# Asking earlier for the last weights of the first expert, and checking the counts later

## The chip, the core and the metric

The kernel runs on one core of one Trainium2 chip. The core has five engines with queues of their own: TensorE (PE in the rows; its weight loads are PEld), VectorE (DVE), ScalarE (ACT), GpSimd (POOL) and SyncE (SP), which here only issues transfers. Each engine takes its instructions in the order in which they were written into its queue, and waits on semaphores for what others produce. The metric is the device time of one execution in microseconds, the median of three runs.

## What is computed

Three stages follow each other, on 3072 tokens of 384 numbers: a linear attention with a decaying state, a gated MLP (`sigmoid(x @ w_gate) * (x @ w_val) @ w_out`), and a mixture of eight experts of which every token takes one. The change lies in the third:

```python
logits = xn @ en.T / tau
expert_idx = np.argmax(logits, axis=1)
gate_w = probs[np.arange(N), expert_idx]
for e in range(E):
    mask = expert_idx == e
    h = np.maximum(x[mask] @ w1[e], 0.0)
    out[mask] = gate_w[mask, None] * (h @ w2[e])
```

`w1[e]` is 384 by 1024 and `w2[e]` 1024 by 384, all in float32.

## The kernel before

Attention and MLP run over groups of 256 tokens. From the second third on two groups are taken together in a "wide" step of 512 columns (L720, L765). When a group's rows of x are done, each row is given an expert and a place in that expert's region of a DRAM buffer `xs`, and GpSimd scatters the rows there (`route_rank`, L837; two scatters of 128 rows for each group). An expert later reads its rows back from `xs` as one block.

The experts come after the last wide step. Their weights lie in DRAM as eight blocks f = 0 to 7 of 128 by 768: 384 columns of w1 and 384 of w2. `load_we` (L851) asks for one block, 384 KB, into one of three buffers `wraw`; `split_we` (L858 to L863) makes of it a high part (ScalarE) and a rest (VectorE), in a tile `we` of the pool `wp`. That pool has 18 places of 6 KB a partition, which held the MLP's weights before and are used anew as these are done with. The call `weights(e, f)` splits block f of expert e + 1 and asks for the block two further on. So a load waits for a free `wraw`, that is for the split three blocks earlier.

The first expert (expert 0) has 448 rows and is computed in pieces, so that the PE need not wait for the last four scatters. Its 320 early rows, which earlier groups filled, are read during the last wide step (tile `first`, `first_rows`): two tiles of 128 rows and one of 64. Their first layer is `first_h` (tiles `hm`, eight blocks f), run right after the last wide step, while the last two groups are ranked and scattered beside it. The second layer of the two whole tiles is `emit_y(0, f, 0)` and `emit_y(0, f, 1)` (L1332). The 64 early rows go through `emit_rest` (L1358): GpSimd adds the two parts of `hm` into `rh` (L1416), and eight products take the plain float32 weights w2 from two tiles `w2f` of 768 KB each, asked for by `load_rest` (L1342). The 128 late rows (tile `x0`, read by the transfer of L1424 after all scatters) are transposed (L1429), copied to `x0T` (L1430) and taken through both layers (L1435, then L1332 with t = 2) with plain float32 weights for the first. Then expert 1 begins, whose rows are the tile `xrow` (`load_rows`, L1277) and are transposed by `do_xT` (L1297).

`verdict` (L1189 to L1209) checks on VectorE whether the counts fit the regions and the decays lie in their range, with one small product on the PE, and writes a flag. A general path is taken at the very end if the flag is set; all engines read it there. SyncE's read of it (`TENSOR_LOAD flag`, L1486) may be placed earlier in its queue by the tile framework, which orders each engine's instructions by priorities of its own.

Of the kernel before, what the change touches and what calls it, by code (L numbers as in the profile page):

```python
# [8 lines left out]
F32 = mybir.dt.float32  # L9
F32R = mybir.dt.float32r  # L10
BF16 = mybir.dt.bfloat16
# [5 lines left out]
ALU = mybir.AluOpType  # L17
AX = mybir.AxisListType

CAP = 448  # L20
# [4 lines left out]
FIRST = 320  # L25
# [21 lines left out]
EMB_T = (-1.29,)  # L47
EMB_AT = 24.35
WARM = 12
VERDICT = 5  # L50
RANK = 1
DOTS = ((2, 3, 3, 2, 0, 0), (4, 4, 4, 4, 4, 4))
WARM_WIDE = 6
# [8 lines left out]
def kernel(  # L62
# [44 lines left out]
    def after_scatters(key, ins):  # L107
        ins = getattr(ins, "ins", ins)
        for q in scatters[key]:
            tc.add_manual_dep(  # L110
                ins, q.name, mybir.DependencyInfo(mybir.DependencyClass.Sync, mybir.DependencyReason.DATA),
                reason="reads what every scatter wrote",
            )

    def follow(ins, before):

        tc.add_manual_dep(
            ins, before.name,
            mybir.DependencyInfo(mybir.DependencyClass.NoSync, mybir.DependencyReason.DATA), reason="order",
        )  # L120
# [181 lines left out]
    if True:  # L302
# [546 lines left out]
        def load_we(e, f):  # L849
# [2 lines left out]
            wraw[e, f] = r  # L852
            last_we[:] = [getattr(q, "ins", q)]

        last_relu = []

        def split_we(e, f):
# [37 lines left out]


        fst = {}
        lim = c1.tile([P, 4, 4], F32, name="lim")
        left = lim[:, 3, 3:4]

        def first_rows():
            assert not dots and not ranks
            cum = cums[LAST % 3]
            pc = ps_a.tile([P, E], F32, tag="a0", name="pc")
            nc.tensor.matmul(pc, ones, cum[:, 0, :], start=True, stop=True)
            nc.vector.tensor_scalar(left, pc[:, 0:1], -1.0, float(FIRST), op0=ALU.mult, op1=ALU.add)
            nc.vector.tensor_scalar(left, left, 0.0, None, op0=ALU.max)
            experts_in_order(pc[0:1, :])
            for t in range(2):
                nc.vector.tensor_tensor(slot0[1][:, t, 0:1], slot0[1][:, t, 0:1], left, op=ALU.add)  # L910
            x = wp.tile([P, 3, RW], F32, tag="w", name="first")
            for a, b, n in ((0, 2, P), (2, 3, FIRST - 2 * P)):
                rows = xs[a * P:a * P + (b - a) * n].rearrange("(t p) c -> p t c", p=n)
                after_scatters("xs", nc.sync.dma_start(out=x[0:n, a:b], in_=rows))
            fst["x"] = x
            for q in range(2):
                r = wp.tile([P, 4, 384], F32, tag="w", name="raw1")
                nc.sync.dma_start(out=r, in_=wex[0, 4 * q:4 * q + 4, :, 0:384].rearrange("f p c -> p f c"))
                fst["w", q] = r
# [245 lines left out]
        for g, f, wide in steps:  # L1165
            if wide == 2:
                for _ in emit_wide(g, f):
                    at_tick()
                    tick += 1
            else:  # L1170
                emit_gv(g, f)
            pend.append((g, f, wide))
            at_tick()
            tick += 1
            drain(LAG if wide == 1 else 1)
            if g == LAST and f < 2:
                load_we(0, f)
            if g == LAST and f >= 2:
                split_we(0, f - 2) if f - 2 < XF else None
                if f < XF:  # L1180
                    load_we(0, f)
                elif f < XF + 2:
                    load_we(1, f - XF)
            if g == LAST and f == AT_ROWS:
                first_rows()
            if g == LAST and f >= 9:
                first_xT(f - 9)
        drain(0)
        def verdict():  # L1189
            q = nc.vector.tensor_scalar(lim[:, 0, :], wd, W_MIN, None, op0=ALU.is_ge)  # L1190
            follow(getattr(q, "ins", q), fst["lo"])
            nc.vector.scalar_tensor_tensor(lim[:, 1, :], wd, W_MAX, lim[:, 0, :], op0=ALU.is_le, op1=ALU.mult)
            nc.vector.tensor_reduce(lim[:, 2, 0:1], lim[:, 1, :], axis=AX.X, op=ALU.add)
            tot = c1.tile([P, E + 2], BF16, name="tot")
            nc.vector.tensor_copy(tot[:, 0:E], cums[NG % 3][:, 0, :])
            nc.vector.tensor_copy(tot[:, E:E + 2], lim[:, 2, 0:1].to_broadcast([P, 2]))
            pf = ps_a.tile([P, E + 2], F32, tag="a0", name="pf")
            nc.tensor.matmul(pf, ones, tot, start=True, stop=True)
            fl = lim[0:1, 3, :]
            nc.vector.tensor_tensor(fl[:, 2:3], pf[0:1, 0:1], left[0:1, :], op=ALU.add)  # L1200
            over = Am0[0:1, 6, 0:E]
            nc.vector.tensor_tensor(over, pf[0:1, 0:E], cape, op=ALU.subtract)
            nc.vector.tensor_reduce(fl[:, 0:1], over, axis=AX.X, op=ALU.max)
            nc.vector.tensor_scalar(fl[:, 0:1], fl[:, 0:1], 0.0, None, op0=ALU.is_gt)
            nc.vector.tensor_scalar(fl[:, 1:2], pf[0:1, E:E + 1], 4.0 * P, None, op0=ALU.is_lt)
            nc.vector.tensor_scalar(fl[:, 2:3], fl[:, 2:3], float(CAP), None, op0=ALU.is_gt)
            nc.vector.tensor_tensor(fl[:, 0:1], fl[:, 0:1], fl[:, 1:2], op=ALU.max)
            nc.vector.tensor_tensor(fl[:, 0:1], fl[:, 0:1], fl[:, 2:3], op=ALU.max)
            nc.vector.tensor_copy(flag, fl[:, 0:1])  # L1209

        tiles = [(g, t, xr) for g, xr in ends for t in range(2)]
        turned = []
        for f in range(XF):
            first_h(f)
            if f == 0:
                turned = [route_turn(xr, t, n) for n, (g, t, xr) in enumerate(tiles)]
            elif f == 1:
                for n, (g, t, xr) in enumerate(tiles):
                    route_logits(xr, t, n, turned[n])
                picks = [route_pick(g, xr) for g, xr in ends]  # L1220
            elif f == 3:
                for p in picks:
                    route_rank(*p)
            elif f == VERDICT:
                verdict()
        ph1.close()


# [58 lines left out]
        def do_xT(e, k):  # L1287
            if k == 0:
                if e % 2 == 0:
                    t = r2p.tile([P, 3072], F32R, tag="r2", name="xk")  # L1290
                else:
                    t = x2p.tile([P, 6 * REGION], F32R, tag="xk", name="xk")
                xk[e] = t[:, 0:6 * CAPS[e]].rearrange("p (k l n) -> p k l n", k=3, l=2)
            pt = ps_t.tile([P, CAPS[e]], F32, tag="t", name="pt2", padded_shape=[P, 512])
            for t, s in enumerate(spans(e)):
                n = tiles[e][t]
                nc.tensor.transpose(pt[:, s], xrow[e][t][:, k * P:(k + 1) * P], ident[:n, :n])  # L1297
            nc.scalar.activation(xk[e][:, k, 0, :], pt, AF.Copy)
            nc.vector.tensor_tensor(xk[e][:, k, 1, :], pt, xk[e][:, k, 0, :], op=ALU.subtract)
# [33 lines left out]
                    yo[e, t], ht[:, a, :], b, start=(f == 0 and n == 0), stop=(f == XF - 1 and n == 2)  # L1333
                )

        rest_w = {}
        rest_h = {}

        def load_rest(e):
            for q in range(2):  # L1340
                w = wp.tile([P, 4, DM], F32, tag="w", name="w2f")
                nc.sync.dma_start(  # L1342
                    out=w,
                    in_=(wex[bass.ds(at[e], 1)] if e else wex[0:1])[:, 4 * q:4 * q + 4, :, 384:768].rearrange(
                        "e f p c -> (e p) f c"
                    ),
                )
                rest_w[e, q] = w

        def parts(e):  # L1350
            return [slice(P // ways[e] * j, P // ways[e] * j + tiles[e][3]) for j in range(ways[e])]
# [65 lines left out]
        for f in range(XF):  # L1417
            emit_y(0, f, 0)
            emit_y(0, f, 1)
            if f < 4:  # L1420
                weights(0, f)
            if f == 1:
                load_rest(0)
        after_scatters("xs", nc.sync.dma_start(out=x0, in_=xs[FIRST:CAP]))  # L1424
        load_rows(1)
        emit_y(0, XF - 1, 3)
        pt = ps_t.tile([P, 3, P], F32, tag="t", name="pt0")
# [22 lines left out]
        for t in range(4):  # L1450
            finish(0, t)

        pend = []

        def drain2(n):
# [7 lines left out]
        for e in range(1, E):  # L1463
            for f in range(XF):
                emit_h(e, f)
                if e < E - 1:
                    pend.append((e, f))
                    weights(e, f)
                    if 3 <= f < 6:
                        do_xT(e + 1, f - 3)  # L1470
                    elif f == 6:
                        do_gate(e + 1, last_relu[-1] if GATE_AFTER else None)
                drain2(LAG)
                if f == 5 and e + 2 < E:
                    load_rows(e + 2)
                if f == 4 and e + 1 in ways:
                    load_rest(e + 1)
# [91 lines left out]
```

## Time and profile before

| | us |
|---|---|
| median of three runs (lowest to highest) | 823.07 (822.88 to 823.72) |
| the profiled execution | 822.97 |
| its span, first to last instruction | 821.0 |
| PE busy | 793.9 (97%) |
| VectorE, ScalarE, GpSimd busy | 508.0, 317.2, 230.3 |
| mean granted TensorE clock | 0.98 |

Times in rows are microseconds from the start of the span; 1.97 us of the execution lie outside it. The PE is busy nearly all the time, so what matters is where it isn't, and at which clock it works. A row of the timeline gives start, duration, engine, line, operation, `out<-in`, shape and count, and in brackets how long the engine sat idle before it and what ended that.

### The profile page before, as it was taken

The page shows a single profiled execution, that of the slowest core. Times are in us where ns is not written, and L with a number is a line of the kernel's source. Part 1 is how long each engine was busy: PE and PEld are TensorE (multiplying, and loading weights), DVE is VectorE, ACT ScalarE, POOL GpSimd, SP SyncE. Part 2 cuts the span into 40 slices and gives each one's busy share as a digit, 9 for nine tenths or more (in the row PEclk, how much of TensorE's full clock was granted, in tenths as well). Part 3 has the DMA queues.
Part 4 walks back from the last instruction along what each step waited for, and adds up shares of the span by engine and source line. Part 5 has one row for each costly group of instructions (what it writes and reads, how often), then busy time and mean ns, then how long its engine had stood idle before and what let it go on. Part 6 is the DMA issues. An engine that isn't in the chain of part 4 may idle for free.

```text
span 821.0 us, 17075 instructions
## 1 busy us (share of the span) xinstructions
PE 793.9 (97%) x6873; PEld 705.6 (86%) x6873; DVE 508.0 (62%) x1234; ACT 317.2 (39%) x660; POOL 230.3 (28%) x256
## 2 busy tenths in 40 slices
PE   7799999999999999999999999999799999999996
PEld 6689998888888888888888888889599989899996
DVE  6999965576456765566566649534275555556640
ACT  5777642212232123122312243223274454565541
POOL 5612155344261516152523210100311211101202
PEclk8699999999999999999999999999999999999999
DMA  8568833222222122121301022420757556465401
GB/s 333 227 253 299 287 120 136 78 68 79 69 78 69 59 88 79 52 75 41 127 9 61 26 64 69 158 71 20 217 166 247 157 186 229 141 209 172 144 1 56
DMA packets 36575, 103.02 MB, mean 125 GB/s; under 512 B 4406, under 2 KB 19462, under 8 KB 33417
## 3 DMA queue, kind: packets, MB, share of 16 engines
q1 hardware_dynamic: 32871, 91.92, 33.3%
q0 software_dynamic: 3616, 9.93, 3.3%
q8 instruction: 56, 0.92, 0.5%
q14 instruction: 30, 0.25, 0.1%
q10 hardware_dynamic: 2, 0.00, 0.0%
HBM read 84.09 MB, written 16.28 MB: 122 GB/s over the span
## 4 chain that ended last, share of the span: by engine, by line
PE 75%; issue 12%; DVE 5%; POOL 3%; DMA 2%; ACT 2%; POOLq 0%; SPq 0%; ACTq 0%; DVEq 0%
PE o L765 17%; PE pval L720 15%; PE pgate L720 15%; PE ph L949 7%; PE y L1332 5%; PE pgv L720 4%; PE py L636 3%; POOL out_dram L1377 2%; PE py L616 1%; DVE x L429 1%; PE py L593 1%; DMA xs<-xr,pi 1%; DMA ldr<-in_att_dram 1%; PE warm L375 1%; PE ph L1435 1%
## 5 line engine op out<-in xcount | busy, mean ns | idle before, releaser
L720 PE MATMUL pgate<-xt,gv 128*128 128x512 f32 x540 | 134.9, 394 | 0.0
L720 PE MATMUL pval<-xt,gv 128*128 128x512 f32 x540 | 134.3, 393 | 0.0
L765 PE MATMUL o<-wo,gth 128*128 128x384 f32 x480 | 125.1, 341 | 0.0
L720 PEld LDWEIGHTS pval<-xt,gv 128*128 128x128 f32 x540 | 100.0, 188 | 21.6
L949 PE MATMUL ph<-xk,we 128*128 128x384 f32 (+6 forms) x576 | 118.0, 352 | 0.0
L720 PEld LDWEIGHTS pgate<-xt,gv 128*128 128x128 f32 x540 | 100.3, 188 | 18.4
L949 PEld LDWEIGHTS ph<-xk,we 128*128 128x128 f32 x576 | 103.4, 191 | 5.9 <-issue 1.2
L785 DVE SCALAR_TENSOR_TENSOR prod<-xr,embb 128x384 f32<-128x384 f32 x160 | 100.1, 626 | 3.8 <-DMA embb<-embd 1.2
L1332 PE MATMUL y<-we,ht 128*128 128x384 f32 (+1 forms) x528 | 101.4, 339 | 0.0
L735 ACT ACTIVATE gth<-sgw 128x512 fp32r<-128x512 f32 x60 | 37.9, 632 | 143.0 <-DVE sgw L733 143.0
L1332 PEld LDWEIGHTS y<-we,ht 128*128 128x128 f32 (+1 forms) x528 | 91.8, 187 | 1.0
L765 PEld LDWEIGHTS o<-wo,gth 128*128 128x128 f32 x480 | 86.3, 188 | 3.9
L729 ACT ACTIVATE sgw<-pgate 128x512 f32<-128x512 f32 x60 | 35.9, 598 | 123.5 <-PE pgate L720 118.7
L765 PE MATMUL o<-wo,gtl 128*128 128x384 f32 x240 | 80.9, 337 | 0.0
L733 DVE TENSOR_TENSOR sgw<-pval,sgw 128x512 f32<-128x512 f32 x60 | 41.3, 689 | 61.4 <-PE pval L720 51.0
L574 POOL TENSOR_TENSOR Am<-near,sd 128x512 f32<-128x512 f32 (+3 forms) x23 | 30.5, 1326 | 153.2 <-DVE sd L562 109.8
L1377 POOL DMA_INDIRECT out_dram<-yo,xrow x26 | 26.3, 1011 | 166.9 <-ACT yo L1374 154.7
L863 DVE TENSOR_TENSOR we<-wraw,we 128x768 fp32r<-128x768 f32 x64 | 61.1, 957 | 18.8 <-ACT we L860 18.3
L954 DVE SCALAR_TENSOR_TENSOR ht<-ph,ht 128x384 fp32r<-128x384 f32 (+1 forms) x56 | 31.8, 568 | 60.8 <-ACT ht L953 60.5
L737 DVE TENSOR_TENSOR gtl<-sgw,gth 128x512 fp32r<-128x512 f32 x60 | 45.3, 754 | 29.5 <-ACT gth L735 29.5
L720 PE MATMUL pgv<-xt,gv 128*128 128x256 f32 x432 | 59.9, 293 | 1.5 <-DVE gv L437 1.5
L860 ACT ACTIVATE we<-wraw 128x768 fp32r<-128x768 f32 x64 | 53.5, 839 | 16.5 <-POOL rh L1416 8.5
(251 smaller groups left out, 1111.4 us busy)
## 6 DMA issues: line engine op xcount, KB each, us to landing
wraw<-in_wex_dram SPq DMA_DIRECT2D x64, 384.0 KB, 3.5
ld<-in_att_dram SPq DMA_DIRECT2D x20, 1152.0 KB, 5.5
raw<-in_wgv_dram SPq DMA_DIRECT2D x12, 768.0 KB, 7.4
w2f<-in_wex_dram SPq DMA_DIRECT2D x10, 768.0 KB, 6.7
xs<-zt SPq DMA_DIRECT2D x8, 750.0 KB, 8.5
raw<-in_wout_dram SPq DMA_DIRECT2D x6, 768.0 KB, 10.6
xrow<-xs SPq DMA_DIRECT2D x6, 600.0 KB, 5.4
ldr<-in_att_dram SPq DMA_DIRECT2D x3, 1152.0 KB, 6.6
```

The lines of the kernel that those rows point to most:

```text
L720: nc.tensor.matmul(pg, a, x[:, k, b, :], start=(n == 0), stop=(n == 8))
L729: nc.scalar.activation(sg, p0, AF.Sigmoid)
L733: nc.vector.tensor_tensor(sg, p1, sg, op=ALU.mult)
L735: nc.scalar.activation(hi, sg, AF.Copy)
L737: q = nc.vector.tensor_tensor(lo, sg, hi, op=ALU.subtract)
L765: nc.tensor.matmul(po[g][t], gt[a][:, ts_], w[:, f % 2, b, :], start=(f == 0 and n == 0), stop=(f == NF - 1 and n == 2))
L785: dots.append(lambda t=t, e=e: nc.vector.scalar_tensor_tensor(prod, xr[:, t, 0:DM], 1.0, embb[0][:, e], op0=ALU.mult, op1=ALU.mult, accum_ ...
L860: q = nc.scalar.activation(w[:, 0:768], r, AF.Copy)
L863: nc.vector.tensor_tensor(w[:, 768:1536], r, w[:, 0:768], op=ALU.subtract)
L949: nc.tensor.matmul(ph, a, x[:, k, b, :], start=(n == 0), stop=(n == 8))
L1332: nc.tensor.matmul(yo[e, t], ht[:, a, :], b, start=(f == 0 and n == 0), stop=(f == XF - 1 and n == 2))
L1377: q = nc.gpsimd.indirect_dma_start(out=out, out_offset=bass.IndirectOffsetOnAxis(ap=xrow[e][t].bitcast(I32)[:, 393:394], axis=0), in_=o, i ...
```

## The change

`load_rest(0)` is called in step f = 10 of the last wide step, not in the first expert after block f = 1. The order of places that tiles get in the pool `wp` changes with it. The late rows' transfer `x0` has an order dependence on the last `load_we` issued, which is the fourth of `weights(0, 0)` to `weights(0, 3)`. `verdict` is cut in two: the three operations on the decays stay behind block f = 5 of `first_h`; the rest, with its product (now in a bank of the second phase's pool `ps_t`), is called at f = 7 of expert 1. The tiles `lim`, `tot` and `over` lie in the pool that lives through the kernel.

```diff
+AT_REST = 10
+VERDICT = 7
...
             if g == LAST and f == AT_ROWS:
                 first_rows()
+            if g == LAST and f == AT_REST:
+                load_rest(0)
...
-            elif f == VERDICT:
-                verdict()
+            elif f == 5:
+                q = nc.vector.tensor_scalar(lim[:, 0, :], wd, W_MIN, None, op0=ALU.is_ge)
+                follow(getattr(q, "ins", q), fst["lo"])
+                nc.vector.scalar_tensor_tensor(lim[:, 1, :], wd, W_MAX, lim[:, 0, :], op0=ALU.is_le, op1=ALU.mult)
+                nc.vector.tensor_reduce(lim[:, 2, 0:1], lim[:, 1, :], axis=AX.X, op=ALU.add)
...
             emit_y(0, f, 1)
             if f < 4:
                 weights(0, f)
-            if f == 1:
-                load_rest(0)
-        after_scatters("xs", nc.sync.dma_start(out=x0, in_=xs[FIRST:CAP]))
+        q = nc.sync.dma_start(out=x0, in_=xs[FIRST:CAP])
+        after_scatters("xs", q)
+        follow(getattr(q, "ins", q), last_we[0])
         load_rows(1)
...
                     if 3 <= f < 6:
                         do_xT(e + 1, f - 3)
+                    elif f == VERDICT and e == 1:
+                        verdict()
```

SyncE's queue before, from the load of block 2 of expert 1 (`wraw_6529`; blocks 3, 4 and 5 are `wraw_6540`, `wraw_6555` and `wraw_6566`) to the late rows:

```order
L851 DMA wraw_6529<-in_wex_dram 128x768
L1486 TENSOR_LOAD flag_101
L1486 ISA x2
L1342 DMA w2f_6542<-in_wex_dram 128x4x384
L851 ISA
L851 DMA wraw_6540<-in_wex_dram 128x768
L1342 DMA w2f_6544<-in_wex_dram 128x4x384
L851 ISA
L851 DMA wraw_6555<-in_wex_dram 128x768
L851 ISA
L851 DMA wraw_6566<-in_wex_dram 128x768
L1424 DMA x0_6502<-xs_69 128x400
```

The same piece of SyncE's queue now, in which blocks 2 to 5 are `wraw_6519`, `wraw_6530`, `wraw_6541` and `wraw_6552`; the first tile `w2f_6172` stands three rows further up, behind block 0:

```order
L861 DMA w2f_6174<-in_wex_dram 128x4x384
L852 ISA
L852 DMA wraw_6519<-in_wex_dram 128x768
L852 ISA
L852 DMA wraw_6530<-in_wex_dram 128x768
L852 ISA
L852 DMA wraw_6541<-in_wex_dram 128x768
L852 ISA
L852 DMA wraw_6552<-in_wex_dram 128x768
L1407 DMA x0_6492<-xs_69 128x400
L1274 ISA
L1274 DMA xrow_6579<-xs_69 120x4x400
```

Both `w2f` transfers moved ahead of blocks 1 and 2, and the read of the flag is gone from here.

The PE's queue before, from the products of the 64 early rows to the late rows' first layer:

```order
L1358 MATMUL y3_6595<-w2f_6542,rh0_6506 64x384 x4
L1358 MATMUL y3_6595<-w2f_6544,rh0_6506 64x384 x4
L1429 MATMUL pt0_6604<-ident_71,x0_6502 128x128 x3
L1435 MATMUL ph0_6610<-x0T_6503,raw1_6034 128x128 x3
L1435 MATMUL ph0_6616<-x0T_6503,raw1_6034 128x128 x3
```

The PE's queue there now:

```order
L1343 MATMUL y3_6581<-w2f_6172,rh0_6496 64x384 x4
L1343 MATMUL y3_6581<-w2f_6174,rh0_6496 64x384 x4
L1414 MATMUL pt0_6590<-ident_71,x0_6492 128x128 x3
L1294 MATMUL pt2_6678<-ident_71,xrow_6579 128x120
L1420 MATMUL ph0_6596<-x0T_6493,raw1_6034 128x128 x3
L1420 MATMUL ph0_6602<-x0T_6493,raw1_6034 128x128 x3
```

One transposition of expert 1's rows (`xrow_6579`) has moved ahead of the late rows' first layer; its three sisters stay where they were.

ScalarE's queue before, at the splits of expert 1's blocks (`we` from `wraw`) among the last blocks of `first_h`:

```order
L860 ACTIVATE we_6526<-wraw_6080 128x768
L860 ACTIVATE we_6537<-wraw_6124 128x768
L953 ACTIVATE hm_6435<-ph1_6448 128x320
L860 ACTIVATE we_6552<-wraw_6529 128x768
L860 ACTIVATE we_6563<-wraw_6540 128x768
```

ScalarE's queue there now:

```order
L874 ACTIVATE we_6516<-wraw_6080 128x768
L967 ACTIVATE hm_6425<-ph1_6438 128x320
L874 ACTIVATE we_6527<-wraw_6124 128x768
L874 ACTIVATE we_6538<-wraw_6519 128x768
L874 ACTIVATE we_6549<-wraw_6530 128x768
```

The split of block 1 has moved behind the last `hm`; its tile `we` now takes the place in the pool that the first `hm` held, so that it waits for the `rh` additions of blocks 0 and 1.

## Rows read from the trace of the kernel before

**Rows 1.** The page: PE's busy share in 40 slices of 20.5 us.

```profile
PE   7799999999999999999999999999799999999996
```

**Rows 2.** Chain of waits that ended last (start, us, what).

```profile
577.14 7.58 DMA xs<-xr,pi
588.83 5.08 DMA x<-xs
```

**Rows 3.** Timeline of PE, 585 to 597 us.

```profile
585.48 1.82 PE L1358 MATMUL y<-w2f,rh 128*64 128x384 f32 x8 [0.23 <-POOL rh L1416]
590.61 2.83 PE L1358 MATMUL y<-w2f,rh 128*64 128x384 f32 x8 [3.32 <-DMA w2f<-in_wex_dram]
593.95 0.55 PE L1429 MATMUL pt<-ident,x 128*128 128x128 f32 x3 [0.51 <-DMA x<-xs]
595.15 1.60 PE L1435 MATMUL ph<-x0T,raw 128*128 128x128 f32 x12 [0.65 <-DVE x0T L1430]
```

**Rows 4.** Stages: us, busy us of PE, PEld, DVE, ACT, POOL; PEclk, DMA share, GB/s.

```profile
540.00:560.00 20.00, 20.00 (x101) 17.46 (x101) 6.19 (x13) 6.05 (x14) 0.00 (x0) 1.00 0.12 37
...
587.30:590.60 3.30, 0.00 (x0) 0.02 (x1) 1.87 (x2) 0.69 (x1) 0.27 (x3) 0.99 0.96 332
590.60:594.00 3.40, 2.88 (x9) 0.89 (x9) 0.00 (x0) 0.49 (x1) 0.04 (x1) 0.50 1.05 305
...
612.00:660.00 48.00, 48.00 (x254) 44.03 (x253) 25.90 (x47) 22.73 (x44) 9.40 (x9) 1.00 0.64 205
```

**Rows 5.** Timeline of POOL, 577 to 588 us.

```profile
577.14 1.50 POOL L837 DMA_INDIRECT xs<-xr,pi  x1 [0.30 <-ACT we L860]
584.90 0.11 POOL L1410 MEMSET c<- 128x9 f32 x1 [6.26 <-DMA xs<-xr,pi]
...
585.11 0.58 POOL L1416 TENSOR_TENSOR rh<-hm 128x64 f32<-128x64 f32 x2
...
585.79 1.69 POOL L1416 TENSOR_TENSOR rh<-hm 128x64 f32<-128x64 f32 x6
```

**Rows 6.** Timeline of SP, 576 to 590 us (transfers issued).

```profile
576.51 0.41 SPq L1342 DMA_DIRECT2D w2f<-in_wex_dram  x1
577.83 0.36 SPq L851 DMA_DIRECT2D wraw<-in_wex_dram  x1
...
586.36 2.30 SPq L851 DMA_DIRECT2D wraw<-in_wex_dram  x2
588.83 0.34 SPq L1424 DMA_DIRECT2D x<-xs  x1
589.38 0.40 SPq L1277 DMA_DIRECT2D xrow<-xs  x1
```

**Rows 7.** Timelines of DVE and ACT, 575 to 590 us.

```profile
575.61 0.14 DVE L1209 CAST flag<-lim 1x1 int32<-1x1 f32 x1
...
586.41 1.58 ACT L860 ACTIVATE we<-wraw 128x768 fp32r<-128x768 f32 x2 [8.54 <-POOL rh L1416]
...
587.29 1.89 DVE L863 TENSOR_TENSOR we<-wraw,we 128x768 fp32r<-128x768 f32 x2 [8.22 <-ACT we L860]
```

**Rows 8.** Line L837's scatters: issue to landing; 20 before 560 us, then the last four.

```profile
DMA to landing us min/median/max: 2.6/2.6/3.9
...
DMA to landing us min/median/max: 2.6/4.3/7.6
```

**Rows 9.** DMA queues, 579 to 581 us: packets, MB, share of 16 engines.

```profile
q1 hardware_dynamic: 404, 0.63, 105.0%
q0 software_dynamic: 1, 0.00, 0.0%
```

**Rows 10.** Reads of an expert's rows, issued at 589.4 and 603.3: KB, us to landing.

```profile
xrow<-xs SPq DMA_DIRECT2D x1, 750.0 KB, 8.2
...
xrow<-xs SPq DMA_DIRECT2D x1, 600.0 KB, 5.4
```

**Rows 11.** Waits of SP's queue, 556 to 600 us (total, times, longest).

```profile
SPq L1486 <- DVE flag L1209: 13.0, 1, 13.0
```

## What I predicted before the run

> **What bounds the kernel now.** First the page: in 40 slices the PE is at nine tenths or more from the third slice to the last but one, except in slice 29, from 575 to 595 us [rows 1]. So only there can much be won. The chain of waits names two transfers in that slice: the last scatter of rows into `xs`, issued at 577.14 and landed 7.58 us later, and the late rows' read `x`, issued at 588.83 and landed 5.08 us later [rows 2]. The PE's timeline shows what they cost: 0.23 us for `rh`, 3.32 us for the second `w2f`, 0.51 us for `x`, 0.65 us for the copy `x0T` [rows 3]. There is a further cost without an idle gap. The first eight records of the 64 rows' products took 1.82 us, the second eight 2.83 us [rows 3], since the granted clock was 0.50 in the stage from 590.6 to 594.0, the lower of its two levels (1.2 of 2.4 GHz), after a stage of 3.3 us with the PE at 0.00 us busy [rows 4]. From the end of the whole tiles' products (585.48 - 0.23 = 585.25) to the late rows' first layer (595.15) pass 9.9 us that hold only 1.82 + 1.82 + 0.55 = 4.2 us of work at full clock.
>
> Why so late? SP sat 13.0 us in its read of the flag [rows 11], written at 575.75 [rows 7]; the first `w2f` went out at 576.51 and block 3 of expert 1's weights at 577.83 [rows 6], beside the last scatter [rows 5]. Twenty earlier scatters landed after 2.6 to 3.9 us; the last one took 7.6 [rows 8]. From 579 to 581 us queue q1 (SP's) moved 404 packets and q0 (the scatters') one [rows 9]. GpSimd's next instruction waits for that landing until 584.90, and the `rh` additions stand behind it [rows 5].
>
> **The change, part by part.**
>
> *The weights `w2f`, 1.5 MB, move to 540 to 560 us.* That stage had the DMA engines at 0.12 [rows 4], and the tiles are first read at 585, so the transfers cost nothing there. On SP blocks 1 and 2 are queued behind them, whose splits come 30 us later or more; should a free place come late, that is the cover. With `w2f` gone, only block 3 runs beside the last scatter. I take 3.3 us for its landing, the middle of 2.6 and 3.9 [rows 8], with 2.6 and 7.58 as ends: 577.14 + 3.3 = 580.4 in place of 584.72.
>
> The Trainium skill, "DMA: Bandwidth & Descriptors", section on queues, rings and completion order, says that each DMA engine goes round its queues packet by packet. By that the scatter would have had its turn beside `w2f`, and taking `w2f` away would free little; the sum would be the slower rival's below. The row of 404 packets against one speaks against it here [rows 9].
>
> *The chain behind the scatter.* GpSimd starts 0.18 us after the landing, 580.6. The first two `rh` end 0.79 us later (585.69 - 584.90), 581.4; the fourth at 582.05, the last at 583.2 [rows 5]. New is that the split of block 1 waits for the first two `rh`, since it inherits the place of an `hm`. Before, only blocks 2 and 3 stood there [rows 7]. A split takes 0.79 us on ACT, and DVE starts 0.88 us after ACT and takes 0.95 [rows 7]: block 1 is done on DVE at 581.4 + 0.88 + 0.95 = 583.25, block 2 at 584.2. These free the buffers for the loads of blocks 4 and 5, issued at 583.3 and 584.25. The late rows follow the second load by 0.5 us and `xrow` follows them by 0.55 (588.83 and 589.38 behind 586.36 + 2.30 - 0.33 = 588.33) [rows 6]: `x` goes out at 584.8, `xrow` at 585.35, each 4.0 us earlier than now. So the extra split costs about a microsecond of the 4.3 that the scatter gives, less what the second `w2f` no longer holds up.
>
> *The 64 rows' products* find weights and `rh` ready (583.2) when the whole tiles end at 585.25. Sixteen records at 1.82/8 us [rows 3] take 3.65 us, until 588.9. The wait of 3.32 us and the microsecond of half clock are gone.
>
> *The late rows* land 5.08 us after issue at most, as with `w2f` ahead of them [rows 2], so by 589.9; with 768 KB less in front I take 4 us, 588.8. Their three transpositions then run from about 588.95 to 589.5, and `x0T` is ready 0.55 us later.
>
> *The new order on the PE.* One transposition of `xrow` now stands between the late rows' transpositions and their first layer. The PE takes its products in order, so the first layer waits for the whole of `xrow`, which before had until 602.8 to land. Its landing took 8.2 us in the crowd of now (750 KB), and 600 KB took 5.4 [rows 10]. By size 5.4 x 750/600 = 6.75; I take that, since without `w2f` the queue is shorter, and keep 5.4 and 8.2 as ends: 585.35 + 6.75 = 592.1 (590.75 to 593.55). One transposition is about 0.2 us, and the first layer starts at 592.3. The copy `x0T` is hidden under this wait. Now it starts at 595.15 [rows 3]: **2.85 us earlier** (1.4 to 4.2). About half of what was removed comes back as this wait, from 589.5 to 592.1.
>
> *The verdict in expert 1.* Its product leaves one full PE stretch for another, net nothing, at most 0.2 us. Some eleven operations of 0.14 us on VectorE [rows 7] come to 1.5 us in a stretch where it is busy 25.9 of 48 us [rows 4]. Were that cover gone, they would delay one split by 1.5 us. SP's read of the flag now waits in expert 1; behind it is a block load, three blocks ahead of use, which waits for a split on VectorE anyway. I cost it at nothing, at most 1 us of a load that has a block's time to spare.
>
> *Behind the first expert* every stage moves with the first layer; the PE is busy 48.00 of 48.00 us from 612 to 660 [rows 4], with no idle time there to swallow the gain. The profiled execution took 822.97 us (span 821.0 and 1.97 outside), 0.1 below the median. 822.97 - 2.85 = 820.1, against the median **820.2**.
>
> **The rivals.**
>
> *The clock falls in the new gap.* The PE would idle some 2.6 us, less than the 3.3 us after which its clock went to 0.50 [rows 4], but not much. Half clock for the rest of such a stage costs by the row 2.83 - 1.82 = 1.0 us, up to 1.8 if the late rows' first layer falls wholly into it: 821.2 to 822.0. For it speaks the closeness, against it that the gap has work on both sides. The Trainium skill, "TensorE: Matmul & The Clock Gate", section on the clock gate, has the slow clock as the default from which activity releases it; the trace agrees, with 0.50 after the idle stage [rows 4].
>
> *`xrow` lands early or the wait is short.* At 5.4 us it lands at 590.75 and the gain is 4.2 us; without any wait the first layer could start at 590.2, 4.95 earlier. 818.1 to 818.9. It needs the 750 KB to go as fast as 600.
>
> *Slower: the scatter is as late as now.* If its 7.58 us belong to itself and not to `w2f`, GpSimd still starts at 584.90. Block 1's split then comes first in a row of three, blocks 4 and 5 go out at 587.55 and 588.5, `x` at 589.05, `xrow` at 589.6; it lands at 596.4 to 597.8, and the PE, which before didn't need it, starts the first layer 1.4 to 2.85 us later, with perhaps a microsecond of half clock: 824.5 to 826.8. The turning point is a landing of the scatter near 583.2, 6.0 us after issue. Against it speak twenty scatters of at most 3.9 us [rows 8] and the packet counts [rows 9].
>
> *Half of it:* the scatter lands after 4.3 to 6.0 us, its median of now or more [rows 8], and the gain is 1.8 to 0: 821.3 to 823.1.
>
> **How the numbers follow.** Forecast as summed 0.53 (819.3 to 821.5); early `xrow` 0.10; clock 0.19; half 0.10; slower 0.08. A measurement of this kernel can tell some 0.2% from no change, 1.65 us: faster is below 821.4. That takes the early case, nearly all of the forecast (0.50) and under half of the clock's (0.08): 0.68. Same: the rest of the clock (0.11), the half (0.10) and an edge of the others: 0.24. Slower 0.08. The range leaves out the slower rival and the far ends: 818.4 to 822.8.
>
> **What would show it.** In the changed profile the last scatter should land in under 4.3 us, GpSimd's memset of `c` start near 580.6, SP issue `x` near 584.8, and PE show no wait for `w2f`, but one of about 2.6 us for `xrow` ahead of the late rows' first layer, which starts near 592.3. The clock in the stretch behind that wait tells the first rival. It is wrong if the scatter still takes over 6 us, if the PE's wait for `xrow` is over 4 us, or if expert 1 shows a wait that it didn't have.

## The result and the profile after

The changed kernel is slower: 831.71 us (median of 5, 830.12 to 831.92) against 823.07 (median of 5, 822.07 to 826.51), ratio 1.0094 with a 95% interval of 1.0071 to 1.0118 (the ratio is taken from all the runs, not from the two medians). Measured once more with the experiments it was 1.0087 (1.0066 to 1.0108). The profiled execution took 830.12 us, its span 828.3 against 821.0.

Two places lost, and one of them was not in the prediction at all.

**Ahead of the first expert's products**, where the change only puts the two `w2f` loads in and takes the end of the verdict with its one small product out, the loss is 4.3 us: the y products begin at 581.08 in place of 576.76. The rows of PE's timeline that bound the wide stage (start, duration), in the kernel before:

```profile
144.32 2.24 PE L720 MATMUL pgate<-xt,gv 128*128 128x512 f32 x9
...
576.76 8.49 PE L1332 MATMUL y<-we,hm 128*128 128x384 f32 x48
```

The changed kernel:

```profile
141.97 2.26 PE L721 MATMUL pgate<-xt,gv 128*128 128x512 f32 x9
...
581.08 8.51 PE L1329 MATMUL y<-we,hm 128*128 128x384 f32 x48
```

From the first wide `pgate` to the y products pass 439.1 us; before, 432.4. So the stage is 6.7 us longer, and the start of the program happened to be 2.35 us shorter in this execution. The costliest groups of the page say which products became slower (busy us, mean ns of one). The kernel before:

```profile
L720 PE MATMUL pgate<-xt,gv 128*128 128x512 f32 x540 | 134.9, 394 | 0.0
L720 PE MATMUL pval<-xt,gv 128*128 128x512 f32 x540 | 134.3, 393 | 0.0
L765 PE MATMUL o<-wo,gth 128*128 128x384 f32 x480 | 125.1, 341 | 0.0
```

The changed kernel:

```profile
L721 PE MATMUL pval<-xt,gv 128*128 128x512 f32 x540 | 137.6, 399 | 0.0
L721 PE MATMUL pgate<-xt,gv 128*128 128x512 f32 x540 | 136.4, 397 | 0.0
L766 PE MATMUL o<-wo,gth 128*128 128x384 f32 x480 | 125.9, 343 | 0.0
```

The same 1560 products, 3.3 + 1.5 + 0.8 = 5.6 us dearer, with no idle time in front of them: no wait, no clock (1.00 over the stage in both), only 2 to 6 ns on each. What did move are the tiles: `lim`, `tot` and `over` now lie in the first pool, so that the weights in `wp` lie 128 bytes further and `xt`, the moving operand of `pgate` and `pval`, 32 bytes.

**In the first expert** the loss is 2.8 us: from the start of the y products to expert 1's first `ph` (606.55 before, 613.67 now) 29.8 us before, 32.6 now. PE's timeline of the changed kernel, the rows that answer to [rows 3]:

```profile
589.52 2.80 PE L1343 MATMUL y<-w2f,rh 128*64 128x384 f32 x16
597.01 0.90 PE L1414 MATMUL pt<-ident,x 128*128 128x128 f32 x3 [4.68 <-DMA x<-xs]
600.49 0.46 PE L1294 MATMUL pt<-ident,xrow 120*128 120x120 f32 x1 [2.58 <-DMA xrow<-xs]
600.75 2.78 PE L1420 MATMUL ph<-x0T,raw 128*128 128x128 f32 x12
...
603.65 2.58 PE L1420 MATMUL ph<-x0T,raw 128*128 128x128 f32 x12
```

The wait for `w2f` is gone, as meant: the 64 rows' products run in one piece. In its place stand 4.68 us for `x` and 2.58 for `xrow`. The first layer begins 19.7 us after the y products; before it was 18.4. And its blocks of 12 take 2.78 and 2.58 us where they took 1.60. The stages say why (columns as in [rows 4]):

```profile
581.00:592.30 11.30, 11.30 (x66) 9.33 (x64) 4.81 (x5) 2.88 (x5) 4.34 (x15) 1.00 0.34 103
592.30:596.00 3.70, 0.02 (x2) 0.00 (x0) 0.00 (x0) 0.49 (x1) 0.00 (x0) 0.96 0.92 263
596.00:600.50 4.50, 0.91 (x4) 0.51 (x4) 0.56 (x1) 0.00 (x0) 0.19 (x1) 0.50 0.83 187
600.50:606.00 5.50, 5.50 (x27) 5.50 (x27) 1.74 (x4) 1.56 (x4) 0.00 (x0) 0.51 0.00 2
```

After the idle stretch the granted clock is 0.50, its lower level (1.2 of 2.4 GHz), until 606. Why `x` is late is read backwards from SP's rows, then GpSimd's, which answer to [rows 6] and [rows 5]:

```profile
591.57 0.34 SPq L1407 DMA_DIRECT2D x<-xs  x1
592.12 0.39 SPq L1274 DMA_DIRECT2D xrow<-xs  x1
```

```profile
581.57 1.40 POOL L838 DMA_INDIRECT xs<-xr,pi  x1 [0.30 <-issue]
586.68 0.10 POOL L1395 MEMSET c<- 128x9 f32 x1 [3.72 <-DMA xs<-xr,pi]
...
586.89 0.59 POOL L1401 TENSOR_TENSOR rh<-hm 128x64 f32<-128x64 f32 x2
```

The last scatter landed 4.9 us after its issue; then came the `rh` additions, then three splits in a row on ScalarE (first row) and VectorE, and only they freed the buffers for blocks 4 and 5 (counted from zero), behind which `x` was ordered:

```profile
587.51 2.31 ACT L874 ACTIVATE we<-wraw 128x768 fp32r<-128x768 f32 x3 [5.80 <-PE y L1329]
...
588.39 1.71 DVE L877 TENSOR_TENSOR we<-wraw,we 128x768 fp32r<-128x768 f32 x1 [5.88 <-ACT we L874]
...
590.03 1.81 DVE L877 TENSOR_TENSOR we<-wraw,we 128x768 fp32r<-128x768 f32 x2
```

The row of ScalarE names PE's y products as what ended its wait, but the first two `rh` end only 0.03 us before it (586.89 + 0.59 = 587.48), and in e12, e1, e4 and e5 the same row names `rh`. On VectorE the first of the three splits takes 1.71 us, the other two 0.95 and 0.94.

Behind the first expert nothing changed: from expert 1's first `ph` to the end pass 214.6 us, before 214.5.

### The profile page after: what moved, and what is told of

The parts are those of the page before. It is cut to its first block, busy times and chain, and to the rows that moved or that the text cites. A ratio compares the mean times of both kernels' runs of the same rounds, so it can differ in the third digit from the quotient of the medians.

```text
span 828.3 us, 17078 instructions
## 1 busy us (share of the span) xinstructions
PE 800.9 (97%) x6873; PEld 709.4 (86%) x6873; DVE 509.4 (61%) x1234; ACT 317.4 (38%) x660; POOL 230.2 (28%) x256
## 4 chain that ended last, share of the span: by engine, by line
PE 74%; issue 12%; DVE 7%; POOL 3%; DMA 2%; ACT 2%; POOLq 0%; SPq 0%; DVEq 0%; ACTq 0%
PE o L766 17%; PE pval L721 16%; PE pgate L721 15%; PE ph L963 7%; PE y L1329 7%; PE pgv L721 4%; PE py L637 3%; POOL out_dram L1362 2%; PE py L617 1%; DVE x L430 1%; PE py L594 1%; DMA xrow<-xs 1%; PE ph L1420 1%; DVE x L429 1%; PE pt L1294 1%
## 5 line engine op out<-in xcount | busy, mean ns | idle before, releaser
L721 PE MATMUL pval<-xt,gv 128*128 128x512 f32 x540 | 137.6, 399 | 0.0
L575 POOL TENSOR_TENSOR Am<-near,sd 128x512 f32<-128x512 f32 (+3 forms) x23 | 30.5, 1327 | 154.5 <-DVE sd L563 111.9
L967 ACT ACTIVATE ht<-ph 128x384 fp32r<-128x384 f32 (+1 forms) x56 | 28.1, 503 | 81.6 <-PE ph L963 77.2
```

The costliest lines, as they stand in the source:

```text
L721: nc.tensor.matmul(pg, a, x[:, k, b, :], start=(n == 0), stop=(n == 8))
```

## The experiments

Theory A: the longer wide stage comes from where the tiles lie. Theory B: from the moved instructions. Theory C: the first expert loses because of the place of `x` behind the weight blocks and of `xrow`'s transposition ahead of the late rows' first layer, the clock with it. The kernel before was timed beside each set; its median there was 824.14, 820.29, 822.78 and 823.23 us, so only ratios are compared between sets (e1 to e4, e5 to e8, e9 to e12, e13 and e14). "Stage" is the time from the first wide `pgate` to the y products, "layer" from there to the late rows' first layer, both from the one profiled execution.

| kernel | shift of wp, xt (bytes) | stage us | layer us | ratio to before (95%) |
|---|---|---|---|---|
| before | 0, 0 | 432.4 | 18.4 | 1 |
| after, again (e12) | 128, 32 | 439.5 | 19.2 | 1.0087 (1.0066 to 1.0108) |
| e1 | 128, 128 | 433.2 | 19.4 | 1.0024 (1.0003 to 1.0045) |
| e2 | 0, 32 | 437.8 | 16.6 | 1.0024 (1.0002 to 1.0045) |
| e7 | 0, 64 | 430.1 | 18.1 | 0.9987 (0.9967 to 1.0006) |
| e8 | 32, 32 | 430.7 | 18.0 | 1.0000 (0.9978 to 1.0021) |
| e9 | 32, 64 | 436.9 | 17.4 | 1.0012 (0.9992 to 1.0033) |
| e13 | 0, 32 (ld 0) | 437.1 | 17.8 | 1.0030 (1.0013 to 1.0047) |
| e14 | 0, 0 (gt 32) | 433.7 | 18.1 | 0.9997 (0.9980 to 1.0013) |
| e3 | 0, 0 | 433.3 | 17.3 | 0.9988 (0.9968 to 1.0009) |
| e4 | 128, 128 | 432.8 | 16.8 | 0.9997 (0.9978 to 1.0016) |
| e10 | 128, 128 | 432.5 | 18.0 | 0.9997 (0.9981 to 1.0014) |
| e6 | 128, 128 | 430.8 | 19.1 | 0.9997 (0.9976 to 1.0018) |
| e5 | 128, 128 | 432.2 | 12.4 | 0.9910 (0.9880 to 0.9940) |
| e11 | 0, 0 | 432.6 | 12.4 | 0.9910 (0.9888 to 0.9932) |

### Where the tiles lie

**e1, the changed kernel with 96 unused bytes:**

```diff
         xp3 = c1.tile([P, 2, 256], F32R, name="xp3")
+        c1.tile([P, 24], F32, name="pad")
```

> The changed kernel with an unused tile of 96 bytes behind the other constants of the first half, so that the tiles behind it (xt, gt, ld, sg, xr) lie 128 bytes behind the places of before, not 32. No instruction moves. The loss of the change was 4.3 us before the first expert's y products and 2.8 us in the first expert. Theory A (the 4.3 us come from where the tiles lie: 32 bytes further, another residue of the address): xt lies as before by 64 and by 128 bytes, pval goes from 399 back to 393 ns, the first expert's y products start near 577 in place of 581, and the whole takes 826 to 828 us. Theory B (they come from the instructions that were moved, wherever the tiles lie): 831 to 832 us and 399 ns.

Its rows of the page:

```profile
L722 PE MATMUL pgate<-xt,gv 128*128 128x512 f32 x540 | 134.9, 394 | 0.0
L722 PE MATMUL pval<-xt,gv 128*128 128x512 f32 x540 | 134.3, 393 | 0.0
```

To the tenth of a microsecond the numbers of before, with every instruction where the change put it. That is theory A; B falls. Against the changed kernel 96 idle bytes are worth 1.0087 or 1.0094 less 1.0024, 5.2 to 5.8 us, each ratio being known to some 0.002, or 1.7 us.

**e2, the kernel before with 32 unused bytes** (the same line with 8 in place of 24):

> The kernel of before with an unused tile of 32 bytes at the same place: xt, gt, ld, sg and xr lie where the changed kernel has them; no instruction moves. Theory A (addresses): pval 399 ns, the first expert's y products start near 581, and the whole takes 827 to 829 us, about 4 to 5 more than before. Theory B (moved instructions): 823 us, 393 ns.

```profile
L721 PE MATMUL pval<-xt,gv 128*128 128x512 f32 x540 | 137.5, 398 | 0.0
L721 PE MATMUL pgate<-xt,gv 128*128 128x512 f32 x540 | 135.1, 394 | 0.0
```

The slower `pval` can be made without the change. Only `pval` slows here, and the total rose by 2.0 us, less than expected: some two fifths of the changed kernel's 5.6 us belong to `pgate` and `o`, which the shift by 32 alone leaves nearly as they were.

**e7 and e8, which rule:** 64 unused bytes at the same place, and 32 in the first pool, so that weights and `xt` move together.

```diff
         xp3 = c1.tile([P, 2, 256], F32R, name="xp3")
+        c1.tile([P, 16], F32, name="pad")
```

```diff
         flag = cst.tile([1, 1], I32, name="flag")
+        cst.tile([P, 8], F32, name="pad")
```

> The kernel of before with an unused tile of 64 bytes at the same place as the earlier 32: xt, gt, ld, sg and xr lie 64 bytes further. If the address modulo 64 decides (32 good, 0 bad): pval 393 ns, from the first wide pgate to the first expert's y products 432 to 434 us, 823 to 824 us. If modulo 128 decides, or the distance between the weights and xt (now 64 bytes off): pval over 396 ns, 437 us or more, 827 us.

> The kernel of before with an unused tile of 32 bytes in the first pool, so that the weights in wp and all that lies behind, xt included, move by 32 bytes together. If xt's own residue decides (0 of 64 is bad): pval 398 ns, 437 to 439 us from the first wide pgate to the y products, 827 us. If the distance between the weights and xt decides (it is that of before): 393 ns, 432 to 434 us, 823 to 824 us.

e7's two sums are 135.4 and 134.1 us, as much as before together. e8 has `xt` at the very address of e2 and of the changed kernel, and its row is that of before:

```profile
L721 PE MATMUL pval<-xt,gv 128*128 128x512 f32 x540 | 134.3, 393 | 0.0
```

So it is not the place of `xt` but its distance from what lies ahead of it, the weights first of all.

**e9, the test from the other side:** the 32 bytes in the first pool and 32 more behind the constants, `xt` at e7's address.

> The kernel of before with 32 unused bytes in the first pool and 32 more behind the constants of the first half: the weights in wp lie 32 bytes further, xt 64 bytes further. The run with 64 bytes alone, where xt lies at the same address, had 395 and 393 ns for pval and pgate and 430.1 us from the first wide pgate to the y products. If the distance between the weights and xt decides (32 of 64 bytes is bad): pval 397 ns or more, 436 to 439 us, 4 to 6 us slower than before. If the place of xt alone decides: 393 to 395 ns, 430 to 433 us, as before.

```profile
L722 PE MATMUL pval<-xt,gv 128*128 128x512 f32 x540 | 137.6, 399 | 0.0
```

At the same place of `xt`, `pval` takes 2.2 us more than in e7 (135.4) once the weights move by 32, and 3.3 more than before. The whole rose by only 1.0 us (-0.7 to 2.7): the slower products are shown, a loss of 4 to 6 us for this kernel is not.

**e13 and e14, which tiles:** 32 unused bytes in a pool of their own, ahead of `xt` or ahead of `gt`.

```diff
+        gap = ph1.enter_context(tc.tile_pool(name="gap", bufs=1))
+        gap.tile([P, 8], F32, name="pad")
         xtp = ph1.enter_context(tc.tile_pool(name="xtp", bufs=2))
```

> The kernel of before with 32 unused bytes between ld and xt: xt, gt, sg and xr move by 32 bytes, ld and the weights stay. If the place of xt against the weights decides: pval 398 or 399 ns, 436 to 439 us from the first wide pgate to the y products, some 4 us slower. If ld decides: 393 ns and 430 to 433 us.

> The kernel of before with 32 unused bytes between xt and gt: gt, sg and xr move by 32 bytes, xt, ld and the weights stay. If the place of xt against the weights decides: pval 393 ns, 430 to 433 us from the first wide pgate to the y products. If gt, the other operand of the output products, counts too: pval 393 ns, but o over 343 ns and 434 us or more.

e13, then e14:

```profile
L722 PE MATMUL pval<-xt,gv 128*128 128x512 f32 x540 | 137.6, 399 | 0.0
```

```profile
L722 PE MATMUL pval<-xt,gv 128*128 128x512 f32 x540 | 134.7, 394 | 0.0
```

`ld` and `gt` are out of it. e13's total rose by 2.5 us, where some 4 were expected. In every kernel of this study where the distance of `xt` from `wp` is off by 32 of 64 bytes (after, e2, e9, e13) `pval` takes 398 or 399 ns and the stage 436.9 to 439.5 us; in all others 393 to 395 ns and 430.1 to 433.7 us. Within a set the stages of e2, e9 and e13 are 3.4 to 5.0 us longer than those of their neighbours at the former distance.

**e12, the changed kernel once more:**

> The changed kernel once more, beside the others on the same chip. Theory (addresses 4 to 6 us, first expert 2 to 4 us): ratio to before 1.008 to 1.011; pval 398 or 399 ns, 437 to 440 us from the first wide pgate to the y products, the first layer 19 to 20 us after them. Rival (the first measurement was a bad place or time): ratio under 1.005.

1.0087, stage 439.5 us, `pval` 399 ns: the first measurement was no accident.

### The first expert

**e3, the weights alone:** before, with `load_rest(0)` in step 10 of the last wide step.

```diff
+            if g == LAST and f == AT_REST:
+                load_rest(0)
...
-            if f == 1:
-                load_rest(0)
```

> The kernel of before with one part of the change alone: the 1.5 MB of weights for the 64 early rows are asked for in step 10 of the last wide step. The verdict stays where it was, and no tile moves. The late rows' read now stands ahead of blocks 4 and 5 of expert 1's weights. Theory A (addresses make the 4.3 us): the first expert's y products start near 577 as before. Theory B: some microseconds later, 827 or more. Theory C (the 2.8 us in the first expert come from the transposition of xrow ahead of the late rows' first layer, and from the slow clock in the gap): here a transposition of xrow stands ahead too, but x is asked for before two weight blocks and so lands earlier; the first layer waits for xrow, 1 to 3 us later than before: 824 to 826. Rival D (the late rows set it, not xrow): the first layer starts 2 us or more earlier than before, 820 to 822.

PE's timeline:

```profile
585.60 2.80 PE L1362 MATMUL y<-w2f,rh 128*64 128x384 f32 x16
593.80 0.86 PE L1312 MATMUL pt<-ident,xrow 120*128 120x120 f32 x3 [4.92 <-DMA xrow<-xs]
594.45 2.78 PE L1437 MATMUL ph<-x0T,raw 128*128 128x128 f32 x12
```

No wait for `x`, but 4.92 us for `xrow`, and the slow clock behind it. The layer starts 17.3 us after the y products, a microsecond earlier than before, where C expected one to three later and D two or more earlier: C has the mechanism, and its price was set too high by two to four microseconds. The total shows no difference.

**e4, `xrow` behind the first layer:** e1 with one dependence more (`late_mm[0]` is the last product of the late rows' first layer).

```diff
+        late_mm = [None]
...
-                nc.tensor.transpose(pt[:, s], xrow[e][t][:, k * P:(k + 1) * P], ident[:n, :n])
+                q = nc.tensor.transpose(pt[:, s], xrow[e][t][:, k * P:(k + 1) * P], ident[:n, :n])
+                if e == 1 and k == 0 and t == 0:
+                    follow(getattr(q, "ins", q), getattr(late_mm[0], "ins", late_mm[0]))
...
-                nc.tensor.matmul(
+                late_mm[0] = nc.tensor.matmul(
```

> The kernel with 96 bytes of padding (first run of this set), and the first transposition of xrow ordered behind the last product of the late rows' first layer; weights, loads and verdict stay as changed. Theory C: without xrow in front, the first layer starts 0.9 us after x landed, 3 us earlier than in the changed kernel and with less time at the lower clock: 2 to 4 us less than its partner with padding alone. Rival D (x itself lands late, at 20 us behind the start of the y products, and what waits for xrow then waits behind the first layer in any case): within 1 us of the partner.

1.0024 becomes 0.9997, 2.2 us less, and the layer starts at 16.8 in place of 19.4: the transposition's place cost two to three microseconds. `x` is still late, and the clock still falls. PE's timeline, then the stages:

```profile
591.62 2.93 PE L1425 MATMUL ph<-x0T,raw 128*128 128x128 f32 x12 [0.65 <-DVE x0T L1420]
```

```profile
586.00:591.60 5.60, 0.94 (x5) 0.50 (x3) 0.56 (x1) 0.49 (x1) 0.19 (x1) 0.75 0.97 240
591.60:597.00 5.40, 5.38 (x29) 5.38 (x30) 1.79 (x5) 1.92 (x6) 0.00 (x0) 0.63 0.34 73
```

**e6, the clock's price:** e4 with 30 products that nobody reads, in that gap.

```diff
+NBUSY = 30
...
+        busy = ps_t.tile([P, 512], F32, tag="t", name="busy")
+        for _ in range(NBUSY):
+            nc.tensor.matmul(busy[:, 0:P], ident, ident, start=True, stop=True)
```

> As the run with 96 bytes of padding and xrow's transposition behind the late rows' first layer, with 30 products of ident by ident (about 4 us of work that nobody reads) on the PE between the 64 rows' products and the late rows' transpositions, that is in the gap in which it waits for x. It measures the clock's price by itself. Theory F (the clock falls because the PE idles there): the granted clock stays at 1.00 through the late rows' first layer, whose blocks of 12 take 1.60 us each in place of 2.93 and 1.95, and the whole is 1.5 to 2.5 us less than without the products. Rival (the clock falls for another reason): blocks as before, and no less time, or up to 1 us more.

```profile
584.98 6.96 PE L1420 MATMUL busy<-ident 128*128 128x128 f32 x60
591.78 0.49 PE L1423 MATMUL pt<-ident,x 128*128 128x128 f32 x3
592.92 1.60 PE L1429 MATMUL ph<-x0T,raw 128*128 128x128 f32 x12 [0.65 <-DVE x0T L1424]
```

The clock stays at 1.00 and the blocks take 1.60 us, as F has it. The Trainium skill, "TensorE: Matmul & The Clock Gate", section "What's actually happening", says that activity releases the slow clock; these rows, in which the gap is filled and the clock doesn't fall, agree. The time did not fall, since the layer starts 2.3 us later than in e4 (19.1 against 16.8). Part of that is the products: the 30 are 60 records and took 6.96 us, not 4, and hold the PE for about 1.1 us after `x` landed. The rest is `x` itself, which in this execution landed about 1.6 us later than in e4 (GpSimd's copy from it starts 16.9 us after the y products, there 15.3); no run shows why. Yet expert 1's first `ph` comes only 0.6 us later (30.5 against 30.0 us after the y products). So the slow clock cost e4 some 1.7 us there, by one profile of each, and idle products are no way to get them back unless they end when `x` lands.

**e5, `x` ahead of the blocks:** e4 without the line that ordered it.

```diff
         after_scatters("xs", q)
-        follow(getattr(q, "ins", q), last_we[0])
         load_rows(1)
```

> As the run with 96 bytes of padding and xrow's transposition behind the late rows' first layer, but the late rows' read x is no longer ordered behind the weight blocks 4 and 5 of expert 1: SP issues it right behind block 3. Theory C (what the first expert waits for is x, since it stands behind two blocks that themselves wait for splits): x goes out some 3 us earlier and lands before the 64 rows' products end, the PE idles for 0.65 us at most, the clock stays at 1.00, and the first layer starts 12.5 to 13.5 us after the y products began in place of 16.8: 818 to 820 us. Rival E (a read of 200 KB takes as long wherever it stands, since it shares the engines with the blocks): the first layer starts at 15 us or later, 821 to 823 us.

SP issued it ahead of block 3 too, not only of 4 and 5. PE's timeline, then SP's, then GpSimd's:

```profile
585.62 2.80 PE L1348 MATMUL y<-w2f,rh 128*64 128x384 f32 x16
588.35 0.55 PE L1418 MATMUL pt<-ident,x 128*128 128x128 f32 x3
589.55 1.60 PE L1424 MATMUL ph<-x0T,raw 128*128 128x128 f32 x12 [0.65 <-DVE x0T L1419]
```

```profile
581.29 0.34 SPq L1412 DMA_DIRECT2D x<-xs  x1
581.89 3.98 SPq L853 DMA_DIRECT2D wraw<-in_wex_dram  x3
```

```profile
577.68 1.41 POOL L839 DMA_INDIRECT xs<-xr,pi  x1 [0.30 <-issue]
581.22 0.10 POOL L1400 MEMSET c<- 128x9 f32 x1 [2.13 <-DMA xs<-xr,pi]
```

No wait but the 0.65 us of the copy, clock 1.00, layer at 12.4 us, and 0.9% less than before: faster than both kernels. The order does two things. `x` doesn't stand behind splits; and while SP waits at `x` for the scatters, no block is sent beside the last one, which lands 3.4 us after its issue (581.22 less the 0.18 by which the memset follows the landing in [rows 2] and [rows 5], against 577.68).

**e10, the same without e4's dependence:**

> The changed kernel with the 96 bytes of padding, and x no longer ordered behind blocks 4 and 5; the transposition of xrow stays where the change put it, ahead of the late rows' first layer. Theory C: x lands in time, but the first layer then waits for all of xrow: it starts 16.5 to 18 us after the y products began (12.35 with xrow's transposition behind it), the clock falls in that gap, and the whole is 4 to 6 us slower than the run with both edits, within 2 us of before. Rival (the order of the loads was all that was wrong): 13 us or less, 6 us faster than before.

```profile
594.37 1.06 PE L1295 MATMUL pt<-ident,xrow 120*128 120x120 f32 x4 [5.43 <-DMA xrow<-xs]
595.23 2.78 PE L1420 MATMUL ph<-x0T,raw 128*128 128x128 f32 x12
```

18.0 us and 0.9997, as in e4: the read's order alone takes back what e1 had lost and gives nothing over before, since the wait for `x` becomes a longer one for `xrow`. It takes both edits; each alone (e4, e10) ends level with before.

**e11, the verdict where it was:** e3 with e4's dependence.

> The kernel of before, its tiles where they were, with only these parts: the weights of the 64 early rows asked for in the last wide step, and xrow's transposition behind the late rows' first layer (x is read ahead of blocks 4 and 5, since nothing orders it behind). The verdict stays where it was before. Theory: the place of the verdict is worth nothing, and this runs as the faster run of before (ratio 0.991): 0.988 to 0.993 of before, first layer 12.4 us after the y products began. Rival (SP's read of the flag holds up x, as it held up the weights before): x goes out at 585 or later, the first layer starts 14 us or more after the y products, ratio 0.994 or more.

0.991 with the verdict in its old place, 0.991 with it in the new one. Its move is worth nothing that shows, with both ratios known to 0.002 or 0.003; its tiles' place was worth 5 us.

## Why the prediction was wrong

*The weights in the last wide step: right.* They cost nothing there that shows (e3's stage is 433.3 us, before 432.4), and the wait of 3.32 us [rows 3] is gone. The 64 rows' products took 2.80 us, not 3.65, which is off the path, as the PE then waits for `x`.

*The verdict: wrong, and about half of the miss.* The working priced its operations, its product and its wait, all near nothing, and e11 bears that out. It did not ask where three small tiles went. Moving them changed the distance between `xt` and the weights, and some 1560 products paid 5.6 us, a term that the sum did not have. No rival had it; a look at the addresses of both kernels would have shown that something moved, though not its price. The other half of the miss lies in the first expert: expert 1's first `ph` came 32.6 us after the y products, where 29.8 - 2.85 = 26.9 were forecast.

*The last scatter: mis-sized.* Taken at 3.3 us, the middle of 2.6 and 3.9 [rows 8], measured 4.9, with a block's load, issued 0.6 us behind it, still beside it. The landing goes with the loads: with nothing beside it 3.2 to 3.4 us (e3, e5, e10, e11), with one block 4.5 to 5.0 (the changed kernel, e12, e1, e4, e6), with `w2f` and a block 5.6 to 7.9 (the kernel before and the six that keep its order). Both queues from 582.0 to 584.4 in the changed kernel (packets, MB, share of 16 engines):

```profile
q1 hardware_dynamic: 75, 0.23, 48.4%
q0 software_dynamic: 53, 0.15, 17.0%
```

The prediction set the rule of the Trainium skill ("DMA: Bandwidth & Descriptors", "Queues, rings and completion order") that a DMA engine goes round its queues against 404 packets to one [rows 9]. Here, with one block, 75 to 53 agree with the rule; in [rows 9] they don't, and no run shows whether the scatter had packets ready then. What came lies between the two: taking `w2f` away freed 2.7 us, not 4.3.

*The chain to `x`: right in kind, 0.7 us short.* From GpSimd's memset to `x` 4.2 us forecast, 4.9 measured. That a split more stood in the row was seen, but it was priced at 0.95 us on VectorE and took 1.71, which is the whole of the 0.7. It runs while GpSimd still does `rh` (until 587.58 + 1.71 = 589.29). All nine kernels in which this split stands beside those additions had 1.70 to 1.72 us for it, and the 64 splits of the kernel before 0.94 to 1.02; no run moved one of the two alone. Whether `x` need stand behind these blocks at all (e5) was not asked. From issue to landing `x` took 5.1 us, not the 4 taken, but `xrow` came later still.

*The new wait for `xrow`: right, and mis-sized.* 6.75 us forecast, 8.3 measured (600.45 less 592.12), just above the upper end of 8.2 [rows 10]. The belief that the queue would be shorter without `w2f` failed: in the ten kernels whose traces give the landing of these 750 KB they took 7.3 to 9.5 us, with `w2f` in the queue or without.

*The sum of these.* Forecast was a layer 15.5 us after the y products (592.3 less 576.76). Later memset 1.8, chain 0.7, `xrow` 1.6: 19.6, and 19.7 was measured.

*The clock: the rival came true, beyond its price.* An idle gap of 2.6 us was foreseen; it became 4.7 and 2.6 with 0.9 us of work between. The first two blocks lost 1.2 + 1.0 = 2.2 us against 1.60 each, over the 1.8 given as its most. That term was priced apart from the longer gap that a later `x` makes.

Apart from the addresses the change stands where the slower rival put it: e1's 1.0024 is 825.0 us on before's 823.07, and the rival's range was 824.5 to 826.8, with a chance of 0.08. Its chain, scatter, three splits, `x`, `xrow`, is the one that ran, but its condition, a scatter as late as before, is not: by its 4.9 us the half rival (4.3 to 6.0 us, 821.3 to 823.1) should have come. The turning point of 6.0 us was wrong, since the later terms and the clock were each short as well. So the time fits the slower rival partly by luck; chances set by the scatter's landing alone left the other terms out.

## What to carry to other kernels

Before predicting a change that moves or adds a tile, compare the addresses of all tiles before and after, above all the distance between a matmul's two operands; a few unused bytes can be worth more than the edit. A small urgent read belongs ahead of the bulk loads on its queue, and when it waits for the transfer that those loads would slow, the wait itself is a gain. When a wait is removed, look at what the engine has next in its order: e4 and e10 each removed one of two waits in a row and gained nothing over before, both together gained 0.9%.

## What the runs showed of the hardware

**The distance of a product's operands.** With `xt` 32 of 64 bytes off its former distance from the weights, a 128x512 `pval` product, `xt` moving, takes 398 or 399 ns in place of 393 to 395 (four kernels against eleven). The Trainium skill, "SBUF — State Buffer", section "Operand start alignment", asks that an operand begin at a multiple of its element size and says that its runs timed nothing; all addresses here meet that, and the time still differs by over 1%. Open is why: no run shows what the two reads contend for, why `pgate` (397 ns) and `o` slow only in the changed kernel, where the weights are moved by 128 as well, and why the totals of e2, e9 and e13 rose by only 1.0 to 2.5 us when their stages were 3.4 to 5.0 us longer than those of their neighbours. No run moved the weights without the constants of the first half that lie behind them, so that the weights are the partner rests on their being the product's other operand. The start of the program varies in single profiles (the first wide `pgate` between 141.3 and 145.0 us, whatever the kernel), which hides such sums.

**VectorE beside GpSimd.** The first split behind the `rh` additions is a fixed piece of work, 128 by 768, and took 1.71 us beside them, 0.95 without them. It stands on the path to `x` in the changed kernel. That VectorE had been idle isn't the reason: before, the first split behind 8.22 us of idle time took 1.02. That the additions are the reason is argued from their running together, not tested.

**The clock makes part of the spread.** The 35 executions of before beside e1 to e4 run from 820.5 to 828.1 us; those with a mean granted clock of 0.982 or more took 820.6 to 823.7, those with 0.975 or less 823.2 to 828.1. The gap behind the first expert's products let the clock fall in some profiles and not in others: behind 3.3 us without work to 0.50 [rows 4], behind 2.2 us in e2, whose order is the same, not at all (1.51 us for each eight of the 64 rows' products). The gap isn't the only such place: e5's profile has 1.00 from 577 to 601 us, and its six runs still go from 811.5 us at a mean clock of 0.989 to 817.0 at 0.978. In that last run, the profiled one, the clock was 0.74 and 0.65 in the first two stretches of 25 us, and in e11's profile 0.80 and 0.79.
